# V computed in the head layout in three column chunks, its tail rows in the fourth column strip, and the attention weights turned in the forward

## The chip, the cores and the metric

The kernel runs on one core of one Trainium2 chip. The metric is the device time of one execution in microseconds (us), lower is better. TensorE (PE) does the matmuls, VectorE (DVE), ScalarE (ACT) and GpSimd (POOL) do the rest, and SyncE (SP) mostly issues DMAs. All data are bf16 with float32 accumulation in PSUM.

## The reference, cut to what matters

A block of layer norm with modulation, segment-recurrent attention with memory, and a gated linear unit (GLU) is run forward and backward; the kernel returns the output and the gradients of all inputs. The part that the change touches is the attention:

```python
B, S, Dm = (1, 2048, 512); H, Dh = (32, 128); M, seg = (8, 32)
mem = mem0
for s in range(n_seg):                                   # 64 segments
    xs = x[:, s * seg_len:(s + 1) * seg_len, :].copy()
    h = jnp.concatenate([mem, xs], axis=1)               # 8 memory + 32 tokens
    q = jnp.einsum('btd,dhe->bhte', h, Wq)
    k = jnp.einsum('btd,dhe->bhte', h, Wk)
    v = jnp.einsum('btd,dhe->bhte', h, Wv)
    scores = jnp.einsum('bhqe,bhke->bhqk', q, k) * scale
    p = _softmax(jnp.where(mask[None, None], scores, -1000000000.0), axis=-1)
    o = jnp.einsum('bhqk,bhke->bhqe', p, v)
    o = jnp.einsum('bhte,hed->btd', o, Wo)
    mem = o[:, :M, :].copy()
    outs.append(o[:, M:, :])
```

Each segment needs the memory that the segment before it wrote, so the 64 segments are a chain. The GLU is `sigmoid(h @ w_gate) * (h @ w_up) @ w_down` with 1792 columns in the middle. The backward needs the attention weights transposed.

## The kernel before, in words

The kernel runs through stages, one after the other: start, attention forward, GLU forward and backward with its weight gradients, attention backward, weight gradients of the attention.

**Attention forward (`phase2`).** One loop pass is one segment of 40 positions. Its first 32 positions (8 memory rows and 24 tokens) depend on the segment before; they are held transposed in `hT` (128 x 4 x 32). The last 8 tokens, the "tail rows", depend on nothing earlier, so those of four segments (a "tile", 32 rows in `hb`) are computed a tile ahead in passes of their own. A pass (`col_pass`, L245) multiplies 32 rows by 512 weight columns in each of four column strips of PE: for each of the four 128-row blocks of D there is one matmul a strip, 16 in all, and the four strips work side by side. Strips 0 to 2 hold heads 3g, 3g+1, 3g+2 of the first 24 heads, strip 3 holds heads 24 to 31. A half pass gives 512 columns to each strip, so two halves make one projection.

In a segment PE runs, in program order, which is pinned: the two halves of k, the two of q, the first half of V, the transposes of k and q (`turns`), the second half of V, the scores of eleven head groups in three parts (`st_exp`, L724, each followed on ACT by its exponential, L726), `vshift` (L749, between the second and the third part), the denominators (`den`, L730) and the product with V (`pv`, L759) part by part, a transposing group for k or q tail rows, the transposes of the attention output, the output projection (`outproj`, at_ps), slot f1, the sum of its halves (at_ft, L240), slot f2, and k of the next segment. ACT copies the memory rows out of at_ft into the next `hT` (L899) while f2 runs. f1 and f2 (`b_pieces`) hold the tail-row halves of the next tile: V in the first segment of a tile, k in the second, q in the third; the fourth has the output projection of the tail rows (`TailRows`, two pieces of 16 matmuls).

V must stand in `Vst` as 96 rows (three heads a group, 32 rows each) by 11 groups. Strips 0 to 2 stand like this already, and POOL copies them over (L814, L817); strip 3 is moved by three small matmuls onto rows 0 to 95 (`vshift`), and DVE copies the result (L752). The tail rows of V come into rows 96 to 119 by six small DMAs of POOL's queue a segment (`v_tails`, L678 and L679).

PSUM has a pool `psp` of five banks that nearly all tiles of the segment share in turn (tag "p"), and three for the scores. Semaphore waits are set by the framework from the tiles that an instruction reads and writes; each engine works its instructions in order.

SP's queue holds, per segment, the stores of k and q rows (L592, L593), transposing DMAs of `Vst` (L833) and of the exponentials, and stores of the attention output and of its transpose.

**GLU weight gradients and weight turning (end of `phase3`).** After the last GLU tile 11 chunks of `out_9` (16 matmuls of 512 columns, L1216) and 32 chunks of `out_7` and `out_8` (16 matmuls of 448 columns, L1301) are left. Between these chunks stand 32 pieces (`p4_weights_setup_pieces`), each of which loads four heads of one attention weight (512 KB, SP's queue, three staging buffers), transposes them on PE in groups of four (tile wtp, L1367 and L1380) and has DVE or ACT copy them to `WoT`, `WvT`, `WkT`, `WqT`. The chunks read rows that are loaded on ACT's queue: HHROWS in groups of 384 columns (768-byte rows), H2ROWS (2 MB, 1 KB rows), then chunks of 448 columns of DGROWS and DUROWS (1.75 MB, 896-byte rows), each into one of two ring buffers when these come free.

Of the kernel before, what the change touches and what calls it, by code (L numbers as in the profile page):

```python
# [40 lines left out]
class K:  # L41
# [43 lines left out]
    def alloc_dram(self):  # L85
        cfg = self.cfg
        NS = cfg.NS
        d = self.dram
        GL = [NS, 128, cfg.G, 128]
        self.MODROW = d("MODROW", [1, 6 * cfg.D], F32)  # L90
        self.H1ROWS = d("H1ROWS", [cfg.S, cfg.D], BF16)
        self.AOA = d("AOA", [NS + 1, cfg.M + cfg.T, cfg.D], BF16)
        self.VT = d("VT", GL, BF16)
        self.OT = d("OT", GL, BF16)
        self.PS = d("PS", GL, BF16)
        self.QST = d("QST", GL, BF16)
        self.KST = d("KST", GL, BF16)
        self.DMOD = d("DMOD", [6, cfg.D], F32)
        self.DX1ROWS = d("DX1ROWS", [cfg.S, cfg.D], F32)
        self.DAROWS = d("DAROWS", [cfg.S, cfg.D], BF16)  # L100
        self.DAOT = d("DAOT", [NS, 128, cfg.DC, cfg.T], BF16)
        self.H2ROWS = d("H2ROWS", [cfg.S, cfg.D], BF16)
        self.HHROWS = d("HHROWS", [cfg.S, cfg.F], BF16)
        self.DGROWS = d("DGROWS", [cfg.S, cfg.F], BF16)
        self.DUROWS = d("DUROWS", [cfg.S, cfg.F], BF16)
        self.DBROWS = d("DBROWS", [cfg.S, cfg.D], BF16)
        self.OSR = d("OSR", GL, BF16)
        self.DQR = d("DQR", GL, BF16)
        self.DKR = d("DKR", GL, BF16)
        self.DVR = d("DVR", GL, BF16)  # L110
        self.DHA = d("DHA", [NS + 1, 32, cfg.D], BF16)
        self.DHB = d("DHB", [NS // 4, 32, cfg.D], BF16)

# [323 lines left out]
    def phase2(self):  # L437
# [13 lines left out]
        with ExitStack() as ctx:  # L451
# [33 lines left out]
            RAs = [{x: ptiles(f"RA{i}" + x, 1, w=9 * 128)[0] for x in ("vkq", "kq")[i]} for i in range(2)]  # L485
            RAs[1]["v"] = RAs[0]["v"]
            RB = {x: ptiles("RB" + x, 1, w=9 * 128)[0] for x in "kq"}
            RBv = ptiles("RBv", 2, w=9 * 128)
# [17 lines left out]
            mem0 = pt.tile([M, D], BF16, name="mem0")  # L506
            with tc.tile_pool(name="p0", bufs=1) as p0:
# [14 lines left out]
                nc.sync.dma_start(mem0[:], io["A_mem0"].rearrange("o m d -> (o m) d"))  # L522
# [12 lines left out]
                place["v"] = self.load_heads(stage(2), Wv, io["A_Wv"])  # L535
# [70 lines left out]
            def b_pieces(t):  # L606

                bt = btails[t] = {}
                RBt = dict(RB, v=RBv[t % 2])

                def proj_b(x, hf):
                    hb = hxs[t][1]
                    pass_half(x, hf, lambda c: hb[:, c, :, :].rearrange("p s q -> p (s q)"), RBt[x], ("dve", "act")[hf])
                    if hf == 1 and x != "v":
                        rows_out(RBt[x], DR[x], t * nseg_t, nseg_t)
# [13 lines left out]
                P = lambda x, hf: (lambda: proj_b(x, hf))  # L629
                T_ = lambda x: (lambda: turn_b(x))  # L630
                d = {(s4, "f%d" % (hf + 1)): [P(x, hf)] for s4, x in enumerate("vkq") for hf in range(2)}
                d.update({(s4 + 1, "turn"): [T_(x)] for s4, x in enumerate("vkq") if x != "v"})
                return d
# [3 lines left out]
            def evac_turned():  # L637
                while evacs:
# [3 lines left out]
            firsts = {x: [f for k in ((s4, "f1"), (s4, "f2"), (s4 + 1, "turn")) for f in first.get(k, [])] + [evac_turned]  # L642
                      for s4, x in enumerate("vkq")}
            slots = {}

# [13 lines left out]
            tail = TailRows(self, sb2, psp, psp, 1, "ao", rows_b, 2, ptag="p")  # L659
# [14 lines left out]
            def v_tails(s):  # L674

                Vst, rb, o = Vsts[s % 2], RBv[(s // nseg_t) % 2], 8 * (s % nseg_t)
                for j in range(3):
                    nc.gpsimd.dma_start(Vst[96 + 8 * j:104 + 8 * j, 0:1024], rb[32 * j + o:32 * j + o + 8, 0:1024])  # L678
                    nc.gpsimd.dma_start(Vst[96 + 8 * j:104 + 8 * j, 1024:1408], rb[96 + o:104 + o, 384 * j:384 * j + 384])  # L679
# [9 lines left out]
            for s in range(NS):  # L689
# [11 lines left out]
                def proj(x, hf, eng):  # L701
                    pass_half(x, hf, lambda c: hT[:, c, :], RA[x], eng)
                    if hf == 1 and x != "v" and s < NS - 1:
                        rows_out(RA[x], DR[x], s, 1)
# [39 lines left out]

                def vshift():
                    sh = ps_f32("sh_ps")
                    shf = sh[:].rearrange("p g x -> p (g x)")
                    for hl in range(3):
                        nc.tensor.matmul(shf[32 * hl:32 * hl + 32, 0:384], lhsT=self.ident[96:128, 96:128],  # L749
                                         rhs=RA["v"][96:128, 384 * hl:384 * hl + 384], start=True, stop=True,  # L750
                                         tile_position=(96, 32 * hl))
                    nc.vector.tensor_copy(Vst[0:96, 1024:1408], shf[0:96, 0:384])  # L752
# [49 lines left out]
                if s == 0:  # L802
# [3 lines left out]
                    place["v"]()  # L806
                    load_wo(2)
                    for k in (1, 2, 3):
                        p1(1, k)
                    for f in firsts["v"]:  # L810
                        f()
                    v_tails(0)
                proj("v", 0, "dve")
                nc.gpsimd.tensor_copy(Vst[0:96, 0:512], RA["v"][0:96, 0:512])  # L814
                turns()
                proj("v", 1, "dve")
                nc.gpsimd.tensor_copy(Vst[0:96, 512:1024], RA["v"][0:96, 512:1024])  # L817
                if s == 0:
                    p1(1, 4)
# [10 lines left out]
                vshift()  # L830
                st_exp(2)
                if s < NS - 1:
# [48 lines left out]
                self.pop_later()  # L881
                nc.sync.dma_start(self.OSR[s], gl3(Ost))
# [74 lines left out]
    def phase3(self):  # L957
# [300 lines left out]
        with ExitStack() as ctx:  # L1258
            op_ = ctx.enter_context(tc.tile_pool(name="p3g_o", bufs=2, reuse_waits="tile"))
            psG = ctx.enter_context(tc.tile_pool(name="p3g_ps", bufs=4, space=PSUM, reuse_waits="tile"))  # L1260
            setup_pieces = self.p4_weights_setup_pieces(ctx)
# [80 lines left out]
    def p4_weights_setup_pieces(self, ctx):  # L1342
        nc, tc, cfg, io = self.nc, self.tc, self.cfg, self.io
        D, DC, H, E = cfg.D, cfg.DC, cfg.H, cfg.E
        HB = 4
        stg = ctx.enter_context(tc.tile_pool(name="p4stage", bufs=1, reuse_waits="tile"))
        sps = ctx.enter_context(tc.tile_pool(name="p4sps", bufs=2, space=PSUM, reuse_waits="tile"))
        pieces = []
        kk = [0]
        slots = [stg.tile([128, DC * HB * E], BF16, name=f"stage{i}") for i in range(2)]  # L1350
        slots = [t[:, :] for t in slots] + [self.flat(self.Wv, 2 * cfg.NT * 448, DC * HB * E)]
        np_ = [0]

        def slot(pat, **kw):
            np_[0] += 1
            return slots[np_[0] % 3].rearrange(pat, **kw)

        def qkv_piece(src_ap, dst, h0):
            def f():
                srcv = src_ap.rearrange("(c p) h e -> p c h e", p=128)  # L1360
                wn = slot("p (c h e) -> p c h e", c=DC, e=E)
                nc.sync.dma_start(wn, srcv[:, :, h0:h0 + HB, :])
                for hi in range(HB):
                    h = h0 + hi
                    tp = sps.tile([128, DC, 128], BF16, name="wtp")
                    for c in range(DC):
                        nc.tensor.transpose(tp[:, c, :], wn[:, c, hi, :], self.ident[:])  # L1367
                    self.evac("dve" if kk[0] % 3 != 2 else "act", dst[:, h, :], tp[:, :, :].rearrange("p c d -> p (c d)"))
                    kk[0] += 1
            return f  # L1370

        def wo_piece(h0):
            def f():
                wov = io["A_Wo"].rearrange("h e d -> e h d")
                won = slot("p (h d) -> p h d", h=HB)
                nc.sync.dma_start(won, wov[:, h0:h0 + HB, :])
                for c in range(DC):
                    tp = sps.tile([128, HB, 128], BF16, name="wtp")
                    for i in range(HB):
                        nc.tensor.transpose(tp[:, i, :], won[:, i, c * 128:(c + 1) * 128], self.ident[:])  # L1380
                    self.evac("dve" if kk[0] % 3 != 2 else "act", self.WoT[:, c, h0 * E:(h0 + HB) * E],
                              tp[:, :, :].rearrange("p i e -> p (i e)"))
                    kk[0] += 1
            return f

        for h0 in range(0, H, HB):
            pieces.append(wo_piece(h0))
        for (src_ap, dst) in ((io["A_Wv"], self.WvT), (io["A_Wk"], self.WkT), (io["A_Wq"], self.WqT)):
            for h0 in range(0, H, HB):
                pieces.append(qkv_piece(src_ap, dst, h0))  # L1390
        return pieces

    def p4_weights_setup_transposes(self):
        with ExitStack() as ctx:
            for f in self.p4_weights_setup_pieces(ctx):
                f()

    def phase4(self):
# [3 lines left out]
        if not hasattr(self, "p4_ctx"):  # L1402
            self.p4_ctx = ExitStack()
            self.p4_weights_setup_begin()
            self.p4_weights_setup_transposes()
# [756 lines left out]
```

## Time and profile before

| what | value |
|---|---|
| median of 3 runs | 3092.27 us (3091.2 to 3092.86) |
| span of the profiled execution | 3090.4 us |
| PE busy | 3001.3 us (97% of the span) |
| DVE, ACT, POOL busy | 1630.0, 1268.9, 1379.6 us |
| mean granted clock of PE | 0.991 |
| DMA | 703.54 MB, mean 228 GB/s |

The span is the time from the first to the last instruction of one profiled execution; the runs are timed apart. The stretches of this execution:

| stage | from, to (us) | length | PE busy |
|---|---|---|---|
| start | 0 to 58.7 | 58.7 | 31.42 |
| attention forward | 58.7 to 984.0 | 925.3 | 914.13 |
| GLU | 984.0 to 1347.4 | 363.4 | 339.67 |
| GLU weight gradients, weight turning | 1347.4 to 1524.5 | 177.1 | 169.02 |
| changeover | 1524.5 to 1538.3 | 13.8 | 6.25 |
| attention backward | 1538.3 to 2534.0 | 995.7 | 989.92 |
| attention weight gradients | 2534.0 to 3090.4 | 556.4 | 550.86 |

Matmuls are pipelined, so the duration of a row holds its fill and drain, and rows overlap a little; the step from one start to the next is the better measure. In a row such as `... [0.64 <-ACT b_colsk L61]` the bracket says how long the engine had been idle before it and which instruction ended that.

### The profile page before, as it was taken

Reading aid. Unit: us, or ns where it says so; the run is one execution under the profiler, and the core shown is the slowest. Engines: PE = TensorE matmul, PEld = TensorE weight load, DVE = VectorE, ACT = ScalarE, POOL = GpSimd, SP = SyncE. Lnnn points to the kernel's source line nnn. Section 1 sums busy time; section 2 is a strip of 40 time slices with the busy share of each in tenths; the row PEclk is TensorE's granted clock in tenths of the full one; section 3 lists DMA queues with packets and bytes.
Section 4 is the critical chain, followed back from the end, with each engine's and each line's share of the span. In section 5 each row is a group of like instructions: output and inputs, shape, how many; then the busy total and the mean of one; then the engine's idle time right before and its main releaser. Section 6 shows DMA issues by size and latency. Waiting matters only on the chain.

```text
span 3090.4 us, 106123 instructions
## 1 busy us (share of the span) xinstructions
PE 3001.3 (97%) x43845; PEld 1831.6 (59%) x43845; DVE 1630.0 (53%) x3799; ACT 1268.9 (41%) x3056; POOL 1379.6 (45%) x2958
## 2 busy tenths in 40 slices
PE   6999999999998899989999999999999999999999
PEld 3666666666665444445577777777777754445455
DVE  4556656665555788732255555555555642322221
ACT  2555555555555433322255555555555530111011
POOL 3666766667766222211244444444444422333322
PEclk8999999999999999999999999999999999999999
DMA  8888788788778899997599999999999998666574
GB/s 299 215 216 202 203 211 215 205 211 216 200 201 261 201 232 230 226 280 246 169 237 245 246 244 242 241 248 242 247 240 246 243 277 282 197 197 220 191 238 147
DMA packets 845992, 703.54 MB, mean 228 GB/s; under 512 B 544354, under 2 KB 717954, under 8 KB 845124
## 3 DMA queue, kind: packets, MB, share of 16 engines
q1 hardware_dynamic: 714196, 486.69, 62.4%
q0 software_dynamic: 60656, 148.64, 15.1%
q10 hardware_dynamic: 70656, 61.41, 6.3%
q8 instruction: 345, 5.65, 0.8%
q14 instruction: 139, 1.14, 0.1%
HBM read 294.93 MB, written 276.35 MB: 185 GB/s over the span
## 4 chain that ended last, share of the span: by engine, by line
PE 86%; DMA 5%; issue 4%; DVE 2%; POOL 1%; SPq 1%; ACT 0%; POOLq 0%; DVEq 0%; ACTq 0%
PE pass_ps L255 18%; PE gps L1952 9%; PE dh_ps L215 8%; PE g_ps L1614 6%; PE gps5o L1966 4%; PE at_ps L223 4%; PE dhq_ps L223 4%; PE gps L1301 3%; PE mm L1145 3%; PE dh_tps L215 3%; PE turn_ps L264 2%; PE dp_ps L1593 2%; PE tps L1526 2%; PE tps L742 2%; PE mm L1105 2%
## 5 line engine op out<-in xcount | busy, mean ns | idle before, releaser
L1952 PE MATMUL gps<-rows,hrows 128*128 128x512 bf16 (+2 forms) x2160 | 417.5, 356 | 0.0
L1952 PEld LDWEIGHTS <-hrows 128*128 128x128 bf16 x2160 | 211.3, 98 | 204.5
L255 PEld LDWEIGHTS <-hT 128*32 128x32 bf16 x6144 | 158.6, 97 | 169.2 <-DMA Wq<-in_A_Wq_dram 6.0
L1658 POOL COPY dOst<-RAd 96x512 bf16<-96x512 bf16 x128 | 75.4, 612 | 312.7 <-DVE RAd L63 312.5
L63 DVE CAST ot<-gps 128x512 bf16<-128x512 f32 (+3 forms) x76 | 48.1, 634 | 288.3 <-PE gps L1952 198.4
L1956 POOL DMA_DIRECT2D out_dram<-ot x108 | 81.4, 753 | 255.4 <-DVE ot L63 140.2
L61 ACT ACTIVATE ot<-gps 128x512 bf16<-128x512 f32 (+3 forms) x75 | 41.3, 551 | 355.1 <-PE gps L1952 216.1
L909 POOL TENSOR_TENSOR Pst<-Pst,rden 120x1408 bf16<-120x1408 bf16 x63 | 159.7, 2534 | 49.4 <-issue 21.8
L61 ACT ACTIVATE dVT<-g_ps 128x512 bf16<-128x512 f32 (+1 forms) x192 | 109.5, 570 | 96.3 <-PE g_ps L1614 95.6
L63 DVE CAST RA0v<-pass_ps 128x512 bf16<-128x512 f32 x128 | 88.6, 692 | 90.4 <-PE pass_ps L255 86.8
L255 PE MATMUL pass_ps<-Wv,hT 128*32 128x512 bf16 x2048 | 134.2, 382 | 0.0
L215 PE MATMUL dh_ps<-WvT,dVT 128*32 128x512 bf16 x2048 | 133.6, 381 | 0.2 <-DVE RBd L63 0.2
L1966 PE MATMUL gps5o<-WoT,rows 128*128 128x512 bf16 x592 | 128.5, 379 | 1.4 <-DMA rows<-OSR 1.4
L255 PE MATMUL pass_ps<-Wq,hT 128*32 128x512 bf16 x2048 | 123.3, 383 | 5.8 <-DMA Wq<-in_A_Wq_dram 5.8
L223 PE MATMUL at_ps<-Wo,OT 128*32 128x256 bf16 x4096 | 124.9, 275 | 3.8 <-DMA Wo<-in_A_Wo_dram 3.6
L255 PE MATMUL pass_ps<-Wk,hT 128*32 128x512 bf16 x2048 | 121.8, 380 | 2.2 <-ACT hT L899 1.1
L1603 DVE SCALAR_TENSOR_TENSOR dS<-dp_ps,Pst_l 128x512 bf16<-128x512 f32 (+1 forms) x192 | 112.1, 640 | 22.1 <-PE dp_ps L1601 22.1
L255 PE MATMUL pass_ps<-WoT,dyT 128*32 128x256 bf16 (+1 forms) x3072 | 122.5, 308 | 0.9 <-ACT dyT L1732 0.9
L223 PE MATMUL dhq_ps<-WqT,dQT 128*32 128x256 bf16 x4096 | 122.9, 273 | 0.0
L215 PE MATMUL dh_ps<-WkT,dKT 128*32 128x512 bf16 x2048 | 122.3, 380 | 0.0
L223 PEld LDWEIGHTS <-dQT 128*32 128x32 bf16 x4096 | 109.6, 97 | 15.8
L223 PEld LDWEIGHTS <-OT 128*32 128x32 bf16 x4096 | 103.9, 97 | 19.7 <-ACT OT L61 8.4
(419 smaller groups left out, 7073.6 us busy)
## 6 DMA issues: line engine op xcount, KB each, us to landing
OSR<-Ost SPq DMA_DIRECT2D x64, 352.0 KB
OT<-OT SPq DMA_DIRECT2D x64, 352.0 KB
VT<-VTr SPq DMA_DIRECT2D x64, 352.0 KB
PS<-Pst SPq DMA_DIRECT2D x64, 352.0 KB
OT_l<-OT SPq DMA_DIRECT2D x64, 352.0 KB
Pst_l<-PS SPq DMA_DIRECT2D x64, 352.0 KB
VT_l<-VT SPq DMA_DIRECT2D x64, 352.0 KB
DVR<-rows_x POOLq DMA_DIRECT2D x64, 352.0 KB, 6.2
```

The lines of the kernel that those rows point to most:

```text
L61: return nc.scalar.activation(out, in_, AF.Copy)
L63: return nc.vector.tensor_copy(out, in_)
L215: self.nc.tensor.matmul(ps[32 * j:32 * j + 32, :], lhsT=lhsT, rhs=w, start=(n < 4), stop=(n >= total - 4), tile_position=(0, 32 * j))
L223: nc.tensor.matmul(ps[32 * j:32 * j + 32, :], lhsT=x[k], rhs=w[k][:, 256 * d:256 * d + 256], start=(n == 0), stop=(n == total - 1), tile_p ...
L255: self.nc.tensor.matmul(ps[32 * j:32 * j + 32, :], lhsT=lhs(c), rhs=rhs, start=(c == 0), stop=(c == DC - 1), tile_position=(0, 32 * j))
L909: nc.gpsimd.tensor_tensor(Pst[0:120, :, :], Pst[0:120, :, :], rden[:, :].unsqueeze(2).to_broadcast([120, G, 128]), op=ALU.mult)
L1145: nc.tensor.matmul(hp[:], lhsT=xT[:, fc, :], rhs=wT[:, fc, :], start=(n == 0), stop=(n == 2 * FC - 1))
L1301: nc.tensor.matmul(ps[:], lhsT=h2r[:, j, c * 128:(c + 1) * 128], rhs=xr[:, j, :], start=(j == 0), stop=(j == NT - 1))
L1603: nc.vector.scalar_tensor_tensor(out=part3(dS, pi), in0=ps[:, 0:n, :], scalar=cfg.scale, in1=part3(Pst, pi), op0=ALU.mult, op1=ALU.mult)
L1614: nc.tensor.matmul(ps[:, j, :], lhsT=lh[:, g * GW:(g + 1) * GW], rhs=rh[:, g * GW:(g + 1) * GW], start=True, stop=True)
L1952: nc.tensor.matmul(ps[:, 0:ng * E], lhsT=hrows[:, tp_, c * 128:(c + 1) * 128], rhs=rows[:, tp_, 0:ng * E], start=(tp_ == 0), stop=(tp_ == ...
L1966: nc.tensor.matmul(pss[gg][:], lhsT=src[0][:, src[1], gg * E:(gg + 1) * E], rhs=dyrows[:, tp_, :], start=(tp_ == order[0]), stop=(tp_ == o ...
```

## The change

V is computed by `v_chunk` in three chunks of 4, 4 and 3 head groups. In each, strips 0 to 2 compute heads 3g, 3g+1, 3g+2 of the groups (the last group has two heads), so the 96 rows come out as `Vst` wants them. `v_evac` has DVE copy them straight from PSUM into `Vst`; in the third chunk DVE copies two groups and ACT the last, which has 64 rows. `vshift`, POOL's two copies, and the row buffers of V are gone. The fourth strip computes the V tail rows of the next tile: in the first three segments of a tile for one head of the three each, 4 groups beside chunk 0 and 4 beside chunk 1; in the fourth segment the last 3 groups, one head beside each chunk. ACT copies them from chunk 0's PSUM tile, DVE from the others. `v_tails` has three DMAs instead of six. The slots f1 and f2 hold only k and q tail rows, in steps of 128 columns a strip, eight to a projection (in the diff: first step, number of steps, engine that copies); the f2 of the third segment is empty. The tail rows' output projection is in pieces of 20 and 12.

After the scores of a segment `weight_turns` transposes eight 128 x 128 blocks of an attention weight (64 pieces in all), DVE copies them in two halves to `wt_rows`, and SP stores these 256 KB to a new DRAM tensor `WT`. At the end of `phase3`, 16 loads of 1 MB (SP's queue, 8 KB rows) bring the turned weights back; the transposes, staging buffers and copies there are gone, and the PSUM pool of that stage has six buffers instead of four. In the start, Wv is loaded in one DMA in its own order, without the placing copies.

The core of the diff:

```diff
+            VCH = ((0, 4), (4, 4), (8, 3))
+            def v_mm(ps, j, c, lhsT, hl, a, n):
+                wc = Wv[:, c, :].rearrange("p (h e) -> p h e", e=E)
+                n = min(n, (H - hl + 2) // 3 - a)
+                nc.tensor.matmul(ps[32 * j:32 * j + 32, 0:n * E], lhsT=lhsT, rhs=wc[:, 3 * a + hl:3 * (a + n - 1) + hl + 1:3, :],
+                                 start=(c == 0), stop=(c == DC - 1), tile_position=(0, 32 * j))
+            def v_evac(eng, dst, ps, a, n):
+                m = n if a + n < G else n - 1
+                self.evac(eng, dst[0:96, a * E:(a + m) * E], ps[0:96, 0:m * E])
+                if m < n:
+                    self.evac("act" if eng == "dve" else "dve", dst[0:64, (a + m) * E:(a + n) * E], ps[0:64, m * E:n * E])
...
+            def v_chunk(s, k):
+                t, s4 = s // nseg_t, s % nseg_t
+                a, n = VCH[k]
+                tail_of = None
+                if t + 1 < NT:
+                    tail_of = (s4,) + VCH[k] if s4 < 3 and k < 2 else (k,) + VCH[2] if s4 == 3 else None
+                ps = psp.tile([128, 512], F32, name="pass_ps", tag="p")
+                hT = get_ht(s)
+                for c in range(DC):
+                    for j in range(3):
+                        v_mm(ps, j, c, hT[:, c, :], j, a, n)
+                    if tail_of:
+                        v_mm(ps, 3, c, hb_rows(t + 1)(c), *tail_of)
+                v_evac("dve", Vsts[s % 2], ps, a, n)
+                if tail_of:
+                    hl, ta, tn = tail_of
+                    tn = min(tn, (H - hl + 2) // 3 - ta)
+                    self.evac(("act", "dve", "dve")[k], RBv[(t + 1) % 2][32 * hl:32 * hl + 32, ta * E:(ta + tn) * E],
+                              ps[96:128, 0:tn * E])
...
+            def weight_turns():
+                x, h = wt_pieces.pop(0)
+                tp = psp.tile([128, 8, 128], BF16, name="wt_ps", tag="p")
+                for i in range(8):
...
+                    nc.tensor.transpose(tp[:, i, :], src, self.ident[:, :])
+                st = sb2.tile([128, 8, 128], BF16, name="wt_rows", bufs=1)
+                for i in range(2):
+                    self.evac("dve", st[:, 4 * i:4 * i + 4, :], tp[:, 4 * i:4 * i + 4, :])
...
+                return lambda: nc.sync.dma_start(dst, st[:].rearrange("p i d -> p (i d)"))
...
+                return {(0, "f1"): [P("k", 0, 4, "dve")], (0, "f2"): [P("k", 4, 2, "act")],
+                        (1, "f1"): [P("k", 6, 2, "dve"), P("q", 0, 2, "dve")], (1, "f2"): [P("q", 2, 2, "act")],
+                        (2, "turn"): [T_("k")], (2, "f1"): [P("q", 4, 4, "dve")], (3, "turn"): [T_("q")]}
...
-                proj("v", 0, "dve")
-                nc.gpsimd.tensor_copy(Vst[0:96, 0:512], RA["v"][0:96, 0:512])
+                v_chunk(s, 0)
                 turns()
-                proj("v", 1, "dve")
-                nc.gpsimd.tensor_copy(Vst[0:96, 512:1024], RA["v"][0:96, 512:1024])
+                v_chunk(s, 1)
+                v_chunk(s, 2)
...
                 st_exp(0)
                 st_exp(1)
-                vshift()
                 st_exp(2)
+                store_wt = weight_turns()
...
+                store_wt()
                 nc.sync.dma_start(self.OSR[s], gl3(Ost))
...
+        HB = 8
+        def load(x, dst, i):
             def f():
+                if x == "o":
+                    nc.sync.dma_start(dst[:, i // HB, :], self.WT[x][:, i // HB, :])
+                else:
+                    nc.sync.dma_start(dst[:, i:i + HB, :], self.WT[x][:, i:i + HB, :])
             return f
...
+        for x, dst in (("o", self.WoT), ("v", self.WvT), ("k", self.WkT), ("q", self.WqT)):
             for h0 in range(0, H, HB):
+                pieces.append(load(x, dst, h0))
         return pieces
```

## The prediction

> **What bounds the kernel now.** First the table by stage (columns: stretch, length, busy time and count of PE, PEld, DVE, ACT, POOL, granted clock, DMA share, GB/s). The change works in two stages: the attention forward (64 segments) and the stage that ends with the GLU's weight gradients, where the attention weights are now turned.
>
> ```profile
> 58.70:984.00 925.30, 914.13 (x17156) 570.70 (x17160) 547.63 (x1388) 485.95 (x1306) 638.54 (x1366) 1.00 0.81 209
> 1347.40:1524.50 177.10, 169.02 (x1196) 95.76 (x1197) 47.54 (x105) 35.94 (x62) 24.81 (x49) 0.99 0.73 237
> ```
>
> PE is busy 99% of the forward and 95% of the other. In a chain this dense a microsecond of PE work, or of waiting that PE cannot fill, is a microsecond of time. So I looked next at one forward segment on PE, then on DVE and ACT. Start, duration, line, tile:
>
> ```profile
> 609.71 1.05 PE L255 MATMUL pass_ps<-Wk,hb 128*32 128x512 bf16 x16
> 610.59 1.90 PE L255 MATMUL pass_ps<-Wk,hT 128*32 128x512 bf16 x32
> 614.04 1.04 PE L255 MATMUL pass_ps<-Wv,hT 128*32 128x512 bf16 x16
> 616.01 1.05 PE L255 MATMUL pass_ps<-Wv,hT 128*32 128x512 bf16 x16
> 616.99 0.59 PE L724 MATMUL st_ps<-qT,kT 128*128 128x120 bf16 x8
> 617.51 0.74 PE L749 MATMUL sh_ps<-RA0v,ident 32*32 32x384 bf16 x3
> 618.67 0.24 PE L730 MATMUL or_ps<-ones,ET 128*128 128x1 bf16 x4
> ```
>
> ```profile
> 615.20 0.69 DVE L63 CAST RA0v<-pass_ps 128x512 bf16<-128x512 f32 x1 [1.10 <-PE pass_ps L255]
> 615.81 0.35 DVE L63 COPY kT<-turn_ps 128x384 bf16<-128x384 bf16 x1
> 617.17 0.69 DVE L63 CAST RA0v<-pass_ps 128x512 bf16<-128x512 f32 x1 [0.31 <-PE pass_ps L255]
> 622.25 0.42 DVE L63 COPY b_colsk<-turn_ps 128x512 bf16<-128x512 bf16 x1 [0.64 <-ACT b_colsk L61]
> 623.74 0.42 DVE L232 TENSOR_TENSOR at_lo<-at_ps,at_hi 128x256 bf16<-128x256 f32 x1 [0.47 <-ACT at_hi L230]
> ```
>
> ```profile
> 609.82 0.20 ACT L899 ACTIVATE hT<-at_ft 128x32 bf16<-128x32 f32 x1 [0.82 <-PE at_ft L240]
> 612.54 0.60 ACT L61 ACTIVATE RA0k<-pass_ps 128x512 bf16<-128x512 f32 x1 [1.13 <-PE pass_ps L255]
> 617.46 1.62 ACT L726 ACTIVATE ET<-st_ps 128x480 bf16<-128x480 f32 x3 [0.55 <-ACT qT L61]
> 621.62 0.59 ACT L61 ACTIVATE b_colsk<-turn_ps 128x512 bf16<-128x512 bf16 x1
> ```
>
> To see: the three exponentials start at 617.46 and run back to back; the second denominators (618.67) follow the second of them by 1.21 us, so from the scores on the segment waits for ACT, and the V shift at 617.51 lies in that wait. And the two copies of b_colsk out of one PSUM tile, ACT until 622.21, DVE from 622.25: when two engines read one PSUM tile here, they take turns.
>
> **V, as matmuls.** A half of 16 matmuls in four strips takes 0.86 us (610.59 to 612.31, where q starts, holds two). The change makes three chunks, of 4, 4 and 3 heads a strip: 0.86 + 0.86 + 0.86×3/4 = 2.37 instead of 1.72, +0.65 a segment. The fourth strip's matmuls, on the next tile's tail rows, go beside these and cost nothing; cover gone, they would cost the 1.72 a tile that they replace. The shift leaves a wait, gain under 0.07.
>
> **V, as copies: the dear part.** In the program as it is built, two ACT copies of each segment wait for a DVE copy out of the same PSUM tile. (1) Chunk 0: DVE copies rows 0 to 95, then ACT the tail rows; chunk 1 takes over that buffer, so PE waits for ACT. DVE ends at 615.20+0.69 = 615.89; ACT, 512 columns at 0.60, runs 615.93 to 616.53; chunk 1 starts at 616.57, not 616.01. ACT's copies of kT and qT queue behind, but are done before the scores need them. (2) Chunk 2: DVE's queue holds chunk 1 (1.16 after its matmuls start, as 614.04 to 615.20: 617.73), chunk 1's tail (0.61 later, the pitch 615.20 to 615.81: 618.34), and chunk 2's first 256 columns (618.95, 0.42 as at_lo: 619.37). Only then may ACT copy the last head's 64x128 (0.20, as hT: 619.61), and the exponentials stand behind that copy on ACT. They start at 619.63 instead of 617.46: **+2.17**, which holds the +0.65 and the 0.56. The scores themselves are ready for them at 616.57+0.86+0.65+0.59 = 618.67.
> The fourth segment of a tile has tails of 384 columns: 0.11 less on ACT, 0.13 on DVE: +1.93. The last tile has no tails: chunk 1 on time, DVE 617.17 and 617.82, done 618.24, ACT until 618.48: +1.04.
> Sum: 45×2.17 + 15×1.93 + 4×1.04 = 97.7 + 29.0 + 4.2 = **+130.9**. Bounds a segment: +0.58 (copies cost nothing; matmuls less shift) and +2.5 (each of six hand-overs 0.05 dearer). I take 2.17: its terms are rows of the same tiles.
>
> The Trainium skill, PSUM — Partial Sum Buffer, "PSUM bank collisions raise a hardware error", asks for guarding by bank and 32-partition quadrant, since engines in different quadrants of one bank may work at once. Tail rows lie in quadrant 3, the others in 0 to 2: by this rule wait (1) need not be, and the sum would be 60×0.5 = 30 us less; the built program waits all the same. No run so far shows quadrants apart.
>
> **Fewer tail passes.** The six halves of V, k, q before each tile become k and q alone. Behind at_ft the second slot shrinks from 0.86 to 0.43 twice and to nothing once; the next k needs hT (ACT, done at 610.02, k at about 610.07 instead of 610.59). 15×(0.43+0.43+0.50) = **−20.4**; zero to −26 (15×2×0.86) as bounds. Tail chunks 20/12 for 16/16 move 0.22 from slot to slot.
>
> **Weights turned in the forward.** Each segment gets 8 transposes (0.46, as other groups of 8), two DVE copies of 0.42, one 256 KB store on SP's queue between the transposing DMA of Pst and OSR's store. The transposes lie in PE's wait for ACT, the copies on DVE (619.37 to 620.2) before the reciprocal, which waits for 618.67+2.17; DMA 0.81 gains 16.8 MB/925 us = 18 GB/s on 209. Next wt_rows copy waits for the store some 13 us later. Cost 0; without cover 0.46+0.84 a segment, +83. POOL loses two copies and three DMA issues of a segment: off the chain, 0. SP's transposing DMA of V now waits for ACT's 64x128 copy; behind it on SP stands that of Pst, which needs the exponentials anyway, so 0, with 0.5 a segment as what a late P would cost the next reader.
>
> **The turning stage.** By group (count, busy sum, mean ns):
>
> ```profile
> L1301 PE MATMUL gps<-Wv,Wk 128*128 128x448 bf16 x512 | 104.4, 352 | 0.0
> L1216 PE MATMUL gps<-Wk,Wv 128*128 128x512 bf16 x176 | 48.9, 389 | 0.7 <-ACT ot L61 0.7
> L1367 PE MATMUL wtp<-ident,stage 128*128 128x128 bf16 x256 | 23.0, 219 | 0.6 <-DMA stage<-in_A_Wk_dram 0.6
> ```
>
> Start to start, L1216 takes 0.2145 and L1301 0.189: 176×0.2145 + 512×0.189 = 134.6 of 177.1; the other 42.5 are transposes and waits. The 16 loads of 1 MB are issued as soon as WoT's memory is free (DVE first writes it at 1353.4), no longer paced by PE, and share the DMA with the rows that the matmuls need (HHROWS, H2ROWS, the first DGROWS; ACT's queue). How they share, window 1358 to 1362 (packets, MB, share):
>
> ```profile
> q10 hardware_dynamic: 907, 0.93, 75.3%
> q1 hardware_dynamic: 859, 0.38, 36.5%
> ```
>
> Equal packets, not equal bytes: 8 KB loads beside 768-byte rows win. Everything the first DGROWS chunk needs is then served after about 16.8/0.41 (MB/us, the mean of the start's loads from 10 to 36 us) = 41, plus 6.6 MB of rows and 1.3 of stores at 0.327 (this window's mean) = 24: 1353.4+65 = 1418, then 512×0.189 = 97 and some 2.5 for matmuls that run cold after a wait (16 took 6.13 us at 1325.85, behind a wait for HHROWS, where 3.43 is normal): about 1517 against 1524.5, **−7**. Bounds +3 and −42.
>
> By the Trainium skill, DMA: Bandwidth & Descriptors, "Rules for kernel authors", 1 MiB and 128 partitions is the shape for bandwidth, which speaks for these loads; its 341 GB/s for 1 MB makes 49 us, an estimate that fits beside 135 us of matmuls, so −42. The row above, of who is served first, speaks against.
>
> Startup (one 4 MB load of Wv for two and a copy; DMA 0.93 there): 0, ±2. Backward: nothing changes.
>
> **Sum.** 130.9 − 20.4 − 7 = +103.5. Span 3090.4 + 103.5 = 3193.9; the runs' median lies 1.87 above the span: **3196**.
>
> **The rivals.**
> Weight stage keeps all: the rows are served in time, −42 instead of −7: 3161. For: row loads are small. Against: equal packets. 0.17.
> Copies overlap: ACT does not come late, forward +0.58×64−20.4 = +17, in all 3102. For: ACT is idle in 47% of the forward; against: b_colsk. 0.08, of which 0.02 for no difference.
> Faster: the weight stage's 42 us outweigh the forward. It decides once a segment's delay is under (42+20.4)/64 = 0.97; at 0.58 the time is 3067. It needs both rivals above. 0.04.
> The clock: PE now waits over 1 us a segment in pieces; the GLU stage, 93% busy, had 0.97. At 0.97 PE's 914 give +27: 3223. 0.08.
> My forecast: 0.63.
> A measurement here tells 0.2%, 6 us, from no change. Range 3155 to 3216: from below the first rival to most of the clock's. Chances: faster 0.04, same 0.02, slower 0.94.
>
> **What would show it.** Right: in a segment after, ACT's tail copy starts as DVE's first ends and chunk 1 follows it; a 64x128 copy on ACT just ahead of the exponentials, idle before it ended by DVE; four segments in about 66.2 us instead of 59.1; the forward about 1036 long. wtp gone, PE waiting for HHROWS and DGROWS, that stage near 170. Wrong: exponentials within 0.6 of the scores; a forward below 960; or PE waiting for wt_rows.

## The result, and the profile after

The changed kernel takes 3196.55 us (median of 4 runs, 3192.9 to 3198.18), the kernel before 3091.73 beside it: 1.0336 times as long, 95% interval 1.0322 to 1.035. The prediction was 3196. The profiled execution spans 3196.1 us (before 3090.4). By stages, in us; the forward is counted from the second half of the first segment's output projection to the last segment's first scores:

| stage | before | after | moved | forecast |
|---|---|---|---|---|
| up to the first segment's output projection | 58.67 | 59.78 | +1.1 | 0 |
| attention forward | 925.75 | 1031.78 | +106.0 | +110.5 |
| GLU | 363.02 | 366.75 | +3.7 | 0 |
| GLU weight gradients, loads of the turned weights | 177.11 | 170.71 | −6.4 | −7 |
| changeover | 13.78 | 13.10 | −0.7 | 0 |
| attention backward and weight gradients | 1552.07 | 1553.98 | +1.9 | 0 |

The same two rows of the table by stage as were shown of before (length, then busy time and count of PE, PEld, DVE, ACT, POOL, then granted clock, DMA share, GB/s):

```profile
59.78:1091.56 1031.78, 937.76 (x18255) 643.46 (x18254) 629.63 (x1604) 502.62 (x1413) 472.51 (x1057) 1.00 0.71 204
1458.31:1629.02 170.71, 140.03 (x685) 68.40 (x689) 13.51 (x21) 11.67 (x21) 24.76 (x49) 0.90 0.72 253
```

PE was busy for 99% of the forward and is now busy for 91% of it. It does 24 us more work there, but 106 us more time pass: most of the loss is waiting. The waits of PE in the forward, after (waiter and what it waited for: us in total, times, longest):

```profile
PE or_ps L803 <- ACT ET L799: 55.9, 62, 1.0
PE pass_ps L653 <- ACT RBv L61: 22.8, 59, 0.4
```

They are the two places of the forecast: the denominators wait for the exponentials, and V's chunk 1 for ACT's copy of tail rows. The waits of ACT there name what is behind both:

```profile
ACT Vst L61 <- DVE Vst L63: 102.3, 62, 1.7
...
ACT RBv L61 <- DVE Vst L63: 58.3, 59, 1.0
```

One segment after, on PE, ACT and DVE, beside the segment of before that starts with k at 610.59:

```profile
659.30 1.91 PE L256 MATMUL pass_ps<-Wk,hT 128*32 128x512 bf16 x32
665.21 0.40 PE L653 MATMUL pass_ps<-Wv,hT 128*32 128x512 bf16 x3 [0.41 <-ACT RBv L61]
666.84 0.75 PE L797 MATMUL st_ps<-qT,kT 128*128 128x120 bf16 x11
667.42 0.61 PE L712 MATMUL wt_ps<-ident,Wq 128*128 128x128 bf16 x8
669.01 0.25 PE L803 MATMUL or_ps<-ones,ET 128*128 128x1 bf16 x4 [0.98 <-ACT ET L799]
```

```profile
664.57 0.59 ACT L61 ACTIVATE RBv<-pass_ps 32x512 bf16<-32x512 f32 x1 [0.99 <-DVE Vst L63]
...
668.23 0.27 ACT L61 ACTIVATE Vst<-pass_ps 64x128 bf16<-64x128 f32 x1 [1.71 <-DVE Vst L63]
668.40 1.37 ACT L799 ACTIVATE ET<-st_ps 128x480 bf16<-128x480 f32 x3
```

```profile
663.85 0.69 DVE L63 CAST Vst<-pass_ps 96x512 bf16<-96x512 f32 x1 [1.03 <-PE pass_ps L653]
...
666.33 0.69 DVE L63 CAST Vst<-pass_ps 96x512 bf16<-96x512 f32 x1 [0.75 <-PE pass_ps L653]
667.05 0.69 DVE L63 CAST RBv<-pass_ps 32x512 bf16<-32x512 f32 x1
667.78 0.42 DVE L63 CAST Vst<-pass_ps 96x256 bf16<-96x256 f32 x1
```

Read it as a relay: DVE copies chunk 0 until 664.54, ACT the tail rows of the same PSUM tile from 664.57, PE may start chunk 1 at 665.21. Then DVE works through chunk 1, its tail rows and chunk 2 in one row, 666.33 to 668.20; ACT has been idle for 1.71 us before it may copy the last head group at 668.23, and the exponentials stand behind that copy. The scores that they need had their first part done long before; the eight weight transposes at 667.42 lie in PE's wait and cost nothing.

In the last stage PE's waits are two loads, where before there were none above 3.9:

```profile
PE gps L1277 <- DMA Wv<-HHROWS: 21.9, 1, 21.9
PE gps L1362 <- DMA Wv<-DGROWS: 8.6, 1, 8.6
```

and the queues in the first of them, window 1480 to 1496 (packets, MB, share of the 16 engines):

```profile
q1 hardware_dynamic: 785, 5.74, 86.8%
q10 hardware_dynamic: 782, 0.60, 11.5%
```

As in the window that was shown of before, the packets of the two queues are nearly equal in number (785 and 782 here, 907 and 859 there); the loads of the weights (q1) get 5.74 MB through while the rows that PE waits for (q10) get 0.60.

### The profile page after: what moved, and what is told of

It is laid out like the page before. It is cut to its first block, busy times and chain, and to the rows that moved or that the text cites. A ratio compares the mean times of both kernels' runs of the same rounds, so it can differ in the third digit from the quotient of the medians.

```text
span 3196.1 us, 107090 instructions
## 1 busy us (share of the span) xinstructions
PE 2996.0 (94%) x44414; PEld 1879.4 (59%) x44485; DVE 1677.6 (52%) x3931; ACT 1260.4 (39%) x3123; POOL 1208.9 (38%) x2638
## 4 chain that ended last, share of the span: by engine, by line
PE 69%; issue 13%; POOL 6%; DMA 5%; DVE 3%; ACT 2%; SPq 1%; another core or an unknown queue 0%; POOLq 0%; ACTq 0%; DVEq 0%
PE gps L1971 10%; PE pass_ps L256 9%; PE dh_ps L216 7%; PE g_ps L1633 6%; PE gps5o L1985 4%; PE dhq_ps L224 3%; PE dh_tps L216 3%; PE mm L1206 3%; PE pass_ps L653 3%; PE at_ps L224 2%; PE dp_ps L1612 2%; PE tps L1545 2%; PE mm L1166 1%; PE mm L1139 1%; PE mm L1143 1%
## 5 line engine op out<-in xcount | busy, mean ns | idle before, releaser
L653 PE MATMUL pass_ps<-Wv,hT 128*32 128x512 bf16 (+2 forms) x2304 | 175.4, 356 | 23.2 <-ACT RBv L61 23.2
L256 PEld LDWEIGHTS <-hT 128*32 128x32 bf16 x4096 | 115.0, 97 | 111.0 <-POOL kT L65 6.8
L63 DVE CAST Vst<-pass_ps 96x512 bf16<-96x512 f32 (+1 forms) x192 | 114.7, 598 | 111.8 <-PE pass_ps L653 109.9
L342 POOL DMA_DIRECT2D AOA<-at_rb x64 | 36.2, 566 | 320.7 <-DVE at_rb L338 320.7
L653 PEld LDWEIGHTS <-hT 128*32 128x32 bf16 x2304 | 91.6, 96 | 71.7 <-issue 22.2
L752 POOL DMA_DIRECT2D Vst<-RBv x192 | 99.9, 525 | 82.2 <-ACT RBv L61 40.5
L653 PE MATMUL pass_ps<-Wv,hb 128*32 128x512 bf16 (+2 forms) x576 | 128.2, 372 | 0.0
```

The lines of the kernel that those rows point to most:

```text
L63: return nc.vector.tensor_copy(out, in_)
L256: self.nc.tensor.matmul(ps[32 * j:32 * j + 32, :], lhsT=lhs(c), rhs=rhs, start=(c == 0), stop=(c == DC - 1), tile_position=(0, 32 * j))
L653: nc.tensor.matmul(ps[32 * j:32 * j + 32, 0:n * E], lhsT=lhsT, rhs=wc[:, 3 * a + hl:3 * (a + n - 1) + hl + 1:3, :], start=(c == 0), stop=( ...
L752: nc.gpsimd.dma_start(Vst[96 + 8 * j:104 + 8 * j, :], rb[32 * j + o:32 * j + o + 8, :])
```

## The experiments

**The new V path alone** (`v_alone`). The weights are turned in the GLU's last stage as before the change, with its pieces, staging buffers and PSUM pools.

```diff
-                store_wt = weight_turns()
...
-                store_wt()
```

> The new V path alone; the weights are turned in the GLU's end as before. My theory (two ACT copies that wait for DVE make the forward long, the turning there is hidden): the forward stays at 1032 us, four segments at 66.05 us, the last stage goes back to 177: about 3203 us. Rival (the transposes, copies and stores of the turning stretch the forward): its 0.46 to 1.3 us a segment goes, forward 950 to 1000, about 3120 to 3175 us.

Measured: 3232.0 us, 1.0439 of before (1.0422 to 1.0457). The rival falls: without the turning the forward is not shorter. But neither did my number hold: the forward is 1062.9 us, 31 longer than with the turning, the last stage 178.2. The difference is in the clock. The table by stage has, for `v_alone`, for the changed kernel, and for a third kernel (`v_warm`, below):

```profile
60.00:1120.00 1060.00, 938.61 (x17705) 633.99 (x17697) 585.48 (x1473) 502.31 (x1408) 471.61 (x1055) 0.96 0.66 182
```

```profile
60.00:1090.00 1030.00, 935.98 (x18233) 642.43 (x18228) 628.35 (x1598) 501.78 (x1409) 472.02 (x1056) 1.00 0.70 204
```

```profile
60.00:1090.00 1030.00, 936.05 (x18218) 642.19 (x18206) 585.84 (x1478) 502.86 (x1413) 473.90 (x1057) 1.00 0.67 188
```

The granted clock is 0.96, 1.00 and 1.00. On PE's timeline of `v_alone`:

```profile
668.42 0.25 PE L803 MATMUL or_ps<-ones,ET 128*128 128x1 bf16 x4 [1.42 <-ACT ET L799]
...
670.45 0.61 PE L815 MATMUL tps<-ident,Ost 128*128 128x128 bf16 x4
```

The wait for the exponentials is 1.42 us, as no transposes lie in it, and two microseconds later four transposes take 0.61 us where the same four take 0.40 in the changed kernel:

```profile
621.09 0.40 PE L815 MATMUL tps<-ident,Ost 128*128 128x128 bf16 x4
```

In the columns of the table by stage, two stretches of 3.41 us of `v_alone`, the first with the whole wait in it, the second right behind it:

```profile
666.80:670.21 3.41, 1.99 (x41) 1.66 (x39) 1.71 (x5) 2.14 (x7) 0.00 (x0) 1.00 0.38 88
670.21:673.62 3.41, 3.41 (x35) 2.17 (x36) 1.86 (x6) 1.78 (x6) 0.06 (x1) 0.50 1.04 237
```

The clock of the second is 0.50. The forward of `v_alone` has 23 such stretches at 0.50, each 3.41 us long, the changed kernel's has one, at its very start; the segments that none of them hits take 16.30, 16.43 or 16.60 us, as long as with the transposes. So the 31 us are the clock's, and the transposes themselves cost nothing.

**The transposes back, unused** (`v_warm`). `v_alone` with the eight transposes in their place, but no copy of them and no store; nothing of them is used.

> v_alone, and the eight transposes a segment behind the scores again, but no copy of their result and no store: nothing of them is used. If v_alone's forward is 31 us longer because PE idles 1.4 us at a stretch and its clock falls behind that, the transposes shorten the gap to 0.98 and the forward is 1032 again, about 3203 us with the weights turned at the end of the GLU stage. Rival (v_alone is longer for another reason, such as the place of buffers in PSUM or DVE's order): the transposes only fill a wait, and the time stays near 3232 us.

Measured: 3203.08 us (1.0351, 1.0337 to 1.0366), the forward 1031.5. The transposes do not only hide in the wait, they keep PE's clock up through it. And as the changed kernel's forward is 1031.8, the copies and the store of the turned weights, which `v_warm` leaves out, cost nothing there.

**The turning alone** (`turn_alone`). V as before the change; the turning in the forward ahead of the output projection, the loads as in the change.

```diff
                 nc.sync.dma_start(self.OSR[s], gl3(Ost))
+                store_wt = weight_turns()
                 at_ps = outproj()
+                store_wt()
```

> The turning in the forward alone, with V computed as before; the eight transposes stand ahead of the output projection, as there is no free stretch of PE behind the scores. My theory: PE is full there, so 64 x 0.46 = +29 us in the forward, -6 in the stage of the loads: about 3114 us. Rival (the turning is what stretches the forward, by the copies and the store too): over 3160 us. If transposes cost nothing: 3085 us.

Measured: 3111.25 us (1.0052, 1.0037 to 1.0067). Four segments take 60.78 us instead of 59.08, +0.43 a segment for transposes of 0.46; the forward is 948.9, 23 longer than before (29 expected), the last stage is 170.8. Where PE has no wait to put them in, the turning costs its transposes, and nothing that can be seen beside them.

**DVE copies the last head group too** (`last_dve`).

```diff
-                    self.evac("act" if eng == "dve" else "dve", dst[0:64, (a + m) * E:(a + n) * E], ps[0:64, m * E:n * E])
+                    self.evac(eng, dst[0:64, (a + m) * E:(a + n) * E], ps[0:64, m * E:n * E])
```

> The changed kernel, but DVE copies V's last head group too, so that no ACT copy stands between DVE and the exponentials. My theory: the exponentials start 0.5 us after the scores' first matmul instead of 1.6, 1.1 us earlier; DVE's reciprocal then comes some 0.25 late behind the copies; 60 segments x 0.85 = -51: about 3143 us. Rival (the forward is long through V's added matmuls and PE's wait at chunk 1 only): within 5 us of 3196.

Measured: 3148.87 us (1.0177, 1.0162 to 1.0193), 48 less than the changed kernel; the forward 986.8, 45 less. On ACT nothing stands ahead of the exponentials any more but the scores:

```profile
573.44 0.38 ACT L61 ACTIVATE qT<-turn_ps 128x96 bf16<-128x96 bf16 x2
574.60 1.40 ACT L799 ACTIVATE ET<-st_ps 128x480 bf16<-128x480 f32 x3 [0.78 <-ACT qT L61]
```

The exponentials start 0.47 us after the scores' first matmul (574.13), 1.56 in the changed kernel (666.84, 668.40). So one ACT copy of 0.27 us carries 45 us of the loss, by what it waits for. It is less than the 51 expected because the first three segments of a tile gain 0.86 us each, the fourth only 0.28.

**Chunk 0 in one copy** (`stage0`). DVE copies all 128 rows into the columns of `OT`, which is free then; POOL copies both parts on.

```diff
+            STAGED = (0,)
...
+                if tail_of and k in STAGED:
...
+                    st = OT[:, 512 * k:512 * k + n * E]
+                    self.evac("dve", st[:, 0:tn * E], ps[:, 0:tn * E])
+                    if tn < n:
+                        self.evac("dve", st[0:96, tn * E:n * E], ps[0:96, tn * E:n * E])
+                    nc.gpsimd.tensor_copy(Vsts[s % 2][0:96, a * E:(a + n) * E], OT[0:96, 512 * k:512 * k + n * E])
+                    nc.gpsimd.tensor_copy(RBv[(t + 1) % 2][32 * hl:32 * hl + 32, ta * E:(ta + tn) * E],
+                                          OT[96:128, 512 * k:512 * k + tn * E])
+                    return
```

> The changed kernel, but chunk 0 leaves PSUM in one DVE copy of all 128 rows, into a buffer that is free then; POOL copies V's rows and the tail rows from there. My theory: ACT's copy out of chunk 0's tile is gone, chunk 1 starts 0.41 us earlier and all behind it too: 60 x 0.41 = -25, about 3171 us. Rival (chunk 1's start does not matter, as the exponentials are held by DVE's queue, which is as late as before): within 5 us of 3196.

Measured: 3162.22 us (1.0215, 1.02 to 1.023), 34 less than the changed kernel; the forward 999.0, 33 less. The rival falls. The gain is more than expected because I had taken PE's printed idle time of 0.41 for the delay: chunk 1 starts 5.42 us after k instead of 5.91, 0.49 earlier (the prediction had 0.56 for this step), the exponentials 8.61 instead of 9.10, and a segment is 0.55 shorter (16.05 instead of 16.60).

**Both waits away** (`mended`): `stage0` for chunks 0 and 1, `last_dve`, and the second half of the turned weights copied after the first reciprocal.

```diff
+            STAGED = (0, 1)
...
+                wt_rest, store_wt = weight_turns()
...
                 recip(0, 2, or2)
+                wt_rest()
```

> The changed kernel with both waits taken away: chunks 0 and 1 leave PSUM in one DVE copy of all rows each (POOL copies on from there), DVE copies the whole of chunk 2, and the second half of the turned weights after the first reciprocal. My theory: what stays is V's three strips (+0.65 a segment) less the shorter tail slots (1.36 a tile), four segments in 59.08 + 4 x 0.6 - 1.36 = about 60.1 us, the forward about 947, in all about 3112 us. Rival (V's path costs more by other means, POOL's copies late for the product with V): above 3130 us.

Measured: 3109.31 us (1.0052, 1.0038 to 1.0067); the forward is 946.65, the last stage 170.9. Of the 106 us, 85 went with the waits. The exponentials start 7.51 us after k, 0.64 later than before (6.87), which is what V's three strips were to cost (0.65); 64 times this, less the 20.4 forecast for the shorter tail slots, makes the 21 that stay.

**The loads paced** (`paced`): one load for two chunks of `out_7` and `out_8`, on ACT's queue instead of SP's; everything else as in the change.

```diff
-                emit_setup()
...
+                        if c % 2 == 1 and setup_pieces:
+                            setup_pieces.pop(0)()
...
-                    nc.sync.dma_start(dst[:, i:i + HB, :], self.WT[x][:, i:i + HB, :])
+                    nc.scalar.dma_start(dst[:, i:i + HB, :], self.WT[x][:, i:i + HB, :])
```

> The changed kernel, but the 16 loads of 1 MB stand on ACT's queue between the copies of the chunks, behind the rows that these need. My theory (equal packets starve the rows): PE's 21.9 and 8.6 us of waiting go for the most part, that stage 170.7 to about 147, in all about 3172 us. Rival (the DMA has too many bytes to move there in any order): within 6 us of 3196.

Measured: 3169.21 us (1.0246, 1.0231 to 1.0261). The stage is 144.6 instead of 170.7, 10 above the 134.6 of its matmuls, with the same bytes. PE's longest waits for loads there:

```profile
PE gps L1361 <- DMA Wv<-DGROWS: 3.9, 1, 3.9
PE gps L1277 <- DMA Wv<-HHROWS: 1.6, 1, 1.6
```

**The loads in rows of 1 KB** (`rows1k`): queue, place and bytes as in the change.

```diff
-        self.WT = {x: d("WT" + x, [128, cfg.H, cfg.D] if x != "o" else [128, cfg.DC, cfg.H * cfg.E], BF16) for x in "qkvo"}
+        self.WT = {x: d("WT" + x, [128, 32, 2 * cfg.D], BF16) for x in "qkvo"}
...
+                    nc.sync.dma_start(dst[:, i:i + HB, :], self.WT[x][:, i:i + HB, 0:512])
```

> The changed kernel, but the turned weights lie in DRAM with gaps, so that the same 16 loads go in 1 KB rows instead of 8 KB; same queue, same place, same bytes. My theory (the DMA serves the queues packet by packet): 1 KB rows leave the others their half, HHROWS comes about 3 us late instead of 21.9, DGROWS about 5; stage 170.7 to about 150, in all about 3176 us. Rival (shares go by bytes or by queue order): smaller rows only make the loads slower, stage 170 to 180, 3196 us or more.

Measured: 3189.14 us (1.0306, 1.0289 to 1.0323); the stage is 163.4. HHROWS comes 6.5 us late instead of 21.9, so smaller packets do leave the rows their share: in the same window of the trace q1 has 3313 packets and q10 2928, with 3.34 and 1.70 MB. But the gain is 7 us, not 21: the slower loads are still under way when DGROWS is wanted, and PE waits 15.7 us for it instead of 8.6. I had not counted that.

**All together** (`best`, `best_again`): `mended` and `paced`.

> Both waits taken away and the loads paced: 3112 - 24 = about 3088 us, if the two add; that is the kernel before within what can be told.

> The same kernel as best, beside turn_paced on one chip with more rounds: 3085 us, 0.2 to 0.3% below the kernel before.

Measured: 3084.59 us (0.9971, 0.9958 to 0.9984), and in a second series 3084.29 (0.997, 0.9959 to 0.9981). The two mends add, and the kernel is 0.3% faster than before. In `best` the transposes (268.10) still cost nothing: they lie between the scores and the first denominators, which follow the exponentials' start by 0.62 us, as in the changed kernel (0.61).

```profile
268.10 0.61 PE L724 MATMUL wt_ps<-ident,Wk 128*128 128x128 bf16 x8
268.61 0.25 PE L815 MATMUL or_ps<-ones,ET 128*128 128x1 bf16 x4
267.99 1.40 ACT L811 ACTIVATE ET<-st_ps 128x480 bf16<-128x480 f32 x3 [1.20 <-issue]
```

**The old V, turned weights and paced loads** (`turn_paced`).

> V as before, the weights turned in the forward ahead of the output projection, the loads paced on ACT's queue: 3111 - 25 = about 3086 us. It tells whether the new V path, mended, is worth its work: if this is below best, V's part has no share in the gain.

Measured: 3084.45 us (0.9974, 0.9964 to 0.9984), the same as `best_again` on the same chip. V's part of the change, even mended, has no share in the gain: what its three strips cost (the forward of `mended` is 20.9 us longer than before) is about what the transposes cost without a wait to hide in (23.2 in `turn_alone`).

## Why the prediction was right

**V's copies.** The steps of the relay, from the start of k in the segment shown (forecast from before, and measured after):

| step | forecast | after |
|---|---|---|
| chunk 1 starts | 5.98 | 5.91 |
| DVE copies chunk 1 | 7.14 | 7.03 |
| its tail rows | 7.75 | 7.75 |
| chunk 2's first groups | 8.36 | 8.48 |
| exponentials | 9.04 | 9.10 |

Errors nearly cancel. DVE's pitch from copy to copy was 0.72 and 0.73, not 0.61, which adds 0.23; but chunk 1 came 0.07 earlier, DVE took it up 0.04 sooner after its start, and from chunk 2's first groups to the exponentials it took 0.62, not 0.68. The exponentials come 2.23 us later than the 6.87 of before; 2.17 was forecast. Each of the two waits is shown by its own experiment (`stage0`, `last_dve`), both by `mended`.

**A tile.** Four segments take 66.05 us (59.08 before), +6.97; the forecast was 8.44 less 1.36, +7.08. The exponentials come a little later than forecast, and the tile is still shorter: what is gained behind them is 1.70 a tile (three times 2.23 and once 1.98, less 6.97), not 1.36. The segments of the last tile are 0.93 longer, forecast 1.04. Most of the gap from 110.5 to 106.0, 3.6 us, lies in the first segment: the sum counts 2.17 for its V, which runs before the stretch begins, and its end is 1.4 shorter.

**Turning hidden.** Held, and better than told: the change's own wait is the cover (`turn_alone` pays 0.43 a segment without it), and in the changed kernel's wait the transposes are worth 29 us through the clock (`v_alone` against `v_warm`). The prediction did not see the second.

**The stage of the loads.** −6.4 for −7, for the reason given: equal packets, then HHROWS and DGROWS late. Both parts of the sum held: the first DGROWS chunk starts 71.9 us into the stage (1458.31, 1530.17), forecast 70.6, and the 512 matmuls from there take 98.9, forecast 99.3. The clock of the stage was 0.90, but the matmuls that ran slowly behind the wait for HHROWS (78 in 20.2 us) cost nothing further, as PE then waited 8.6 us for DGROWS anyway. `paced` shows what the loads' place was worth, 26 us; with −32.5 against before it still falls short of the rival's −42.

**The clock as a rival.** It did not come in the changed kernel (1.00 in the forward), but `v_alone` shows that it was near.

**Not forecast.** The GLU is 3.7 us longer, with no instruction of it changed; it varies from 363.0 to 367.1 among the kernels here, and I have not found why. That the total came within 1 us is luck: the stages that were to stay as they are add 6.0 us, the forward grew by 4.5 less than forecast, and the runs lie from 3192.9 to 3198.18. The rule on PSUM quadrants stays untried: in every kernel here the waits go by tile, so no run has two engines read different quadrants of one bank at once.

## What to carry to other kernels

Before handing two parts of one PSUM tile to two engines, look at what else stands in the second engine's queue: the copy cost here not its 0.27 us, but all that the first engine had queued ahead of its own part. Work moved into another stage is free only in a wait of PE that stays. In the mended kernel one does, the time between the scores and the first denominators, and the transposes fill it. In the kernel before the V shift fills it, so in `turn_paced` they must be paid. Early loads are not free either: large rows on one queue took the DMA from small rows on another here, and the same loads on the consumers' queue, behind their rows, were worth 26 us.

## What the runs showed of the hardware that I had not expected

A wait of PE of about 1.4 us in each segment was enough to lower its clock: in `v_alone` segments with the same waits took 16.60 or 18.12 us, 16.43 or 17.98, 16.30 or 17.5, about every second or third segment the longer, while with waits of 0.98 (the changed kernel, `v_warm`) they took 16.6, 16.4 and 16.3 nearly every time. The Trainium skill, TensorE: Matmul & The Clock Gate, Part 1, calls the window that decides free-running and 3.4 us long, which fits that the stretches at 0.50 are 3.41 us long each and that some segments are hit and others not. Its section "Why this matters for your kernels" warns of idle gaps above some 3 us; here gaps of half that length, with one of 0.41 some 3 us ahead, cost 31 us of the forward's 1063. In `v_alone` a stretch at 0.50 followed 22 of the 44 waits of 1.40 to 1.43 us and one of the 14 waits of 1.29 (a tile's fourth segment); in `v_warm`, with waits of 0.82 to 1.04, one in the whole forward.
